# Local attention with a leaky feed-forward layer on one core: sixteen weight combinations put right behind the attention visits, their stores on another queue, and operands computed earlier at the start of a pair

## The chip, the cores and the metric

The kernel runs on one core of a Trainium2 chip. The metric is the device time in microseconds (us) of one execution; lower is better. A profiled execution has a span, from its first to its last instruction, and a time of its own, a little longer than the span.

## The reference

Attention within chunks of 64 positions, for 8 batches, 8 heads, 576 positions and a head dimension of 64, and behind it a feed-forward layer (512 to 2048 to 512) with a leaky rectifier of one slope per hidden unit:

```python
scores = scale * np.matmul(q_c, k_c.transpose(0, 1, 2, 4, 3))      # in each chunk of 64
scores = scores - np.max(scores, axis=-1, keepdims=True)
attn = np.exp(scores)
attn = attn / (np.sum(attn, axis=-1, keepdims=True) + 1e-09)
out = np.matmul(attn, v_c)
...
x = out.transpose(0, 2, 1, 3).reshape(B * S, H * D)                # 4608 tokens x 512
h = x @ w_in
g = np.maximum(h, 0.0) + alpha * np.minimum(h, 0.0)
return g @ w_out
```

All data are float32.

## The kernel before

**Tiling.** The 4608 tokens are nine blocks of 512. One "sub" of attention is 128 tokens (two chunks, all heads), so a block needs four subs, 36 in all. To keep float32 accuracy with a faster matmul, each operand is split into a high and a low part (cast on ScalarE, subtraction on VectorE), and each product takes three passes: high x high, high x low, low x high.

**Two ways for the feed-forward layer.** The first three blocks (PLAIN) are computed plainly: 48 steps, one per block and hidden tile of 128 units. A step is twelve matmuls of 128x128x512 for the first product (`ffn_in`, L318), the rectifier `prelu` (L308, L309 on ScalarE, L310 on VectorE), the split of its result (L330, L331), and twelve matmuls for the second product (`ffn_out`, L343), which run a step or two later. Blocks 0 and 1 are done in turns, so their sums leave PSUM in the middle and are added to a partial sum in DRAM later. The other six blocks go as three pairs, each by a Strassen-like scheme with seven products of half size instead of eight: `first_product` (L598) for eight hidden tiles j, then `second_product` (L714) with seven groups i of eight operands.

**Combinations.** That scheme needs sums and differences of quarters of the weights. `combine(side, j, early)` makes them for `w_in` ("wi") and `w_out` ("wo"), eight hidden tiles each, so sixteen calls. A call adds the parts of two split weights into two tiles "t1" (L499), does four half-width additions on them (L506 to L509), splits the two results (L515 on ScalarE, L516 on VectorE) into staging buffers, and stores four halves of 256 KB to DRAM with `keep_a` (L477), from where the pairs stream them back later (`stream`, L536, on GpSimd's queue). The staging buffers are taken in turn from "raw" (two) and "more" (one); with `early` true only from "raw". "more" is also needed by two of the four copies at a block's end.

**Order of the work.** The combinations run in the loop over the 48 steps. A half-step is the place before `ffn_in(n)` (2n) or behind it (2n + 1). `COMBINE` lists the steps n of the sixteen calls, all at 2n. `visits` lists the half-steps of attention: a visit computes the values of an older sub (L279) and the scores (L201) and softmax (L217 to L225) of a new one; then `attn_blocks` transposes its probabilities on VectorE into a tile with one buffer (L232) and eight stores on SyncE's queue rearrange it into "pT" (L239). Loads of v (L170) also go there. Combinations are held behind the softmax of the visit emitted last by `issue_after`, on VectorE and on ScalarE.

A planner puts each engine's instructions in order from the program's order, priorities and its own estimate of the times; on the chip each engine then runs its list in that order. `high_priority(offset=HIGH)` lets instructions go ahead of HIGH (300) others. TensorE's instructions keep the program's order from step 20 on.

**A block's end.** `store` copies four PSUM banks (L372) into "more" (two halves), "ob" and "g", and adds them to the partial sums in DRAM with accumulating stores on GpSimd's queue (L377). TensorE needs the banks again for the next block. Such ends lie at half-steps 52 and 66.

**A pair's second product.** Its operands are made by `operand(g, at)`, at = 0 to 55: a value or difference of the pair's activations, split (`split`, L554 and L555) into two buffers, which for at % 4 are "t1" twice (0), the halves of "more" (1), or "gh" and "gl" (2 and 3). They are made AHEAD (2) places before their use; the first two are made ahead of the last first product. `first_product` uses "gh" and "g" for sums, and "gl" for the input (L630) of two of its last activations.

Of the kernel before, what the change touches and what calls it, by code (L numbers as in the profile page):

```python
# [10 lines left out]
F32R = mybir.dt.float32r  # L11
# [16 lines left out]
def tile_local_attention_prelu_ffn(  # L28
# [12 lines left out]
    nc = tc.nc  # L41
    P = 128
# [9 lines left out]
    TB = 512  # L52
# [4 lines left out]
    JF = NF // 2  # L57
    EARLY = 2 * SPB
    TURNS = (3, 9)
    HIGH = 300  # L60
# [5 lines left out]
    gp = ctx.enter_context(tc.tile_pool(name="gp", bufs=2))  # L66
    stage = ctx.enter_context(tc.tile_pool(name="stage", bufs=2))
# [5 lines left out]
    def f32(t):  # L73
        return t.bitcast(F32)
# [77 lines left out]
    stages = {}  # L152
# [319 lines left out]
        at = ORDERS[side].index(i)  # L472
        return divmod(7 * j + at if side == "wi" else JF * at + j, 2)

    def keep_a(side, i, j, a):
        n, u = unit(side, i, j)
        nc.gpsimd.dma_start(out=units[side][n][:, u], in_=f32(a))  # L477

    halves = (slice(0, 2 * P), slice(2 * P, 4 * P))

# [10 lines left out]
    def combine(side, j, early):  # L491

        ws = wi if side == "wi" else wo
        pair = [ws[j], ws[JF + j]]
        left, right = halves
        a = []
        for w in pair:
            t = stage.tile([P, 512], F32, name="t1")
            nc.vector.tensor_tensor(t, f32(w[:, 0]), f32(w[:, 1]), op=ALU.add)  # L499
            a.append(t)  # L500
        a11, a22 = a[0][:, left], a[1][:, right]
        if side == "wi":
            a12, a21 = a[0][:, right], a[1][:, left]
        else:
            a21, a12 = a[0][:, right], a[1][:, left]
        nc.vector.tensor_tensor(a22, a21, a22, op=ALU.add)  # L506
        nc.vector.tensor_tensor(a21, a11, a21, op=ALU.subtract)
        nc.vector.tensor_tensor(a11, a22, a11, op=ALU.subtract)
        nc.vector.tensor_tensor(a12, a12, a11, op=ALU.subtract)  # L509
        names = ((2, 4), (3, 1)) if side == "wi" else ((2, 3), (4, 1))  # L510
        for t, name in zip(a, names):
            which = "raw" if early else ("raw", "raw", "more")[fetched[0] % 3]
            fetched[0] += 1
            w = stage.tile([P, 2, 512], F32R, name=which, bufs=2 if which == "raw" else 1)
            nc.scalar.copy(w[:, 0], t)  # L515
            nc.vector.tensor_tensor(w[:, 1], t, f32(w[:, 0]), op=ALU.subtract)  # L516
            for half, s in zip((left, right), name):
                keep_a(side, {1: 5, 2: 6, 3: 7, 4: 3}[s], j, w[:, :, half])

    sequence = [(side, n) for _ in range(NPAIR) for side in ("wi", "wo") for n in range(7 * JF // 2)]  # L520
    ring = []
# [130 lines left out]
    def operand(g, at):  # L652
        i, j = ORDERS["wo"][at // JF], at % JF
        b11, b12, b21, b22 = pieces(g, j)
        if i == 7:
            t = gp.tile([P, TB], F32, name="g")
            with tc.issue_after(behind[0][1].ins):
                nc.vector.tensor_tensor(t, b22, b12, op=ALU.subtract)
        else:
            t = {1: b11, 3: b22, 2: b21}.get(i, b12)  # L660
        if at % 4 == 1:
            both = stage.tile([P, 2, TB], F32R, name="more", bufs=1)
            hi, lo = both[:, 0], both[:, 1]
        else:
            pool, names = (stage, ("t1", "t1")) if at % 4 == 0 else (gp, ("gh", "gl"))
            hi, lo = (pool.tile([P, TB], F32R, name=name) for name in names)
        behind[:] = behind[1:] + [split(t, hi, lo)]
        return hi, lo

    def second_product(g, b, operands, conversion, end):  # L670
# [24 lines left out]
        for i in ORDERS["wo"]:  # L695
# [8 lines left out]
            for j in range(JF):  # L704
                at = JF * ORDERS["wo"].index(i) + j
                if at + AHEAD + EARLIER < 7 * JF:
                    difference(g, at + AHEAD + EARLIER)
                if at + AHEAD < 7 * JF:
                    operands.append(operand(g, at + AHEAD))
                hi, lo = operands.pop(0)  # L710
                w = weight("wo", i, j)
                for m in range(2):
# [36 lines left out]
        for n, name in enumerate(("xh", "xl")):  # L749
            x[b + n] = xp.tile([P, NK, TB], F32, name=name)  # L750

    COMBINE = (20, 22, 23, 24, 26, 29, 30, 31, 33, 35, 36, 37, 39, 40, 41, 43)
    combined = [(side, j) for side in ("wi", "wo") for j in range(JF)]
    ops, conversion = {}, []
    for n, (p, b, f) in enumerate(steps):
# [25 lines left out]
        if ready < NF:  # L781
            prepare(ready, done_x.get({2: SPB, 3: SPB + 2, 4: SPB + 3}.get(ready)))
            ready += 1
        elif n in COMBINE:

            with tc.issue_after(stages["softmax"][0].ins), tc.issue_after(stages["softmax"][1].ins):
                combine(*combined.pop(0), n in (23, 24, 25, 26, 32, 33, 34))
        if n == len(steps) - 8:
            ops, conversion = convert(PLAIN)
        if len(steps) - 8 <= n < len(steps) - 4:  # L790
# [1 line left out]
        pending.append((acc, ffn_in(x[b], f), f, f0, f1, b, False))  # L792
        if 2 * n + 1 in late:
            visit(*late[2 * n + 1])
        if n >= len(steps) - 3:

            with tc.issue_after(stages["split"][0].ins):
                for _ in range(3):
                    conversion.pop(0)()
# [12 lines left out]
    for pair in range(NPAIR):  # L812
        b = PLAIN + 2 * pair
        more = pair + 1 < NPAIR
        if more:
            new_raw(b + 2)
        g = {}
        for j in range(JF):
            if more:
                new += 1  # L820
                visit(new - 2, new if new < NSUB else None)
            if j == JF - 1:
                operands = [operand(g, at) for at in range(AHEAD)]
            first_product(ops, g, j)
        if more:
            ops, conversion = convert(b + 2)
        second_product(g, b, operands, conversion, not more)
# [39 lines left out]
```

## Time and profile before

| | before |
|---|---|
| median of 3 runs | 848.83 us (847.81 to 851.46) |
| profiled execution, its own time | 848.08 us |
| its span | 846.3 us |
| mean granted TensorE clock | 0.988 |
| TensorE (PE) busy | 808.6 us (96%) |
| VectorE (DVE) busy | 670.9 us (79%) |
| ScalarE (ACT) busy | 545.5 us (64%) |
| GpSimd (POOL) busy | 213.0 us (25%) |
| DMA moved | 192.40 MB, mean 227 GB/s |

How to read it: L12 is line 12 of the kernel before. A row of a group gives line, engine, operation, written and read tiles, count, durations. A row of waits gives who waited, then what released it, the total in us, how often, and the longest. A row in order of time gives the start, the duration and the instruction; in brackets the engine's idle time before it and what ended it. "SPq", "ACTq" and so on are the engines' sequencers, here where they issue DMAs. "Issue" is time in which an engine waited for nothing that the profile shows. A DMA's row gives the KB of each and the median us from issue to landing. "t" in the rows is a staging tile ("t1", or "t3" for the transposed probabilities).

The first 40 us load and compute the first attention block; the plain blocks with visits and combinations run to about 349 us; the three pairs follow, with their second products from 437, 608 and 765 us.

### The profile page before, as it was taken

Reading aid. Unit: us, or ns where it says so; the run is one execution under the profiler, and the core shown is the slowest. Engines: PE = TensorE matmul, PEld = TensorE weight load, DVE = VectorE, ACT = ScalarE, POOL = GpSimd, SP = SyncE. Lnnn points to the kernel's source line nnn. Section 1 sums busy time; section 2 is a strip of 40 time slices with the busy share of each in tenths; the row PEclk is TensorE's granted clock in tenths of the full one; section 3 lists DMA queues with packets and bytes.
Section 4 is the critical chain, followed back from the end, with each engine's and each line's share of the span. In section 5 each row is a group of like instructions: output and inputs, shape, how many; then the busy total and the mean of one; then the engine's idle time right before and its main releaser. Section 6 shows DMA issues by size and latency. Waiting matters only on the chain.

```text
span 846.3 us, 15382 instructions
## 1 busy us (share of the span) xinstructions
PE 808.6 (96%) x5248; PEld 646.1 (76%) x5248; DVE 670.9 (79%) x1267; ACT 545.5 (64%) x1392; POOL 213.0 (25%) x339
## 2 busy tenths in 40 slices
PE   4699999999798999999989999999999999999998
PEld 4567888777576778777767877777887888888886
DVE  5798999978797987676778997676789966568875
ACT  6976676656666767678775564877766546556552
POOL 3006222224244331111111242111122421112232
PEclk8999999999899999999999999999999999999999
DMA  9729787558678667687774789876567995555778
GB/s 274 212 76 332 242 257 262 175 169 214 192 234 225 203 215 259 215 259 258 255 260 149 242 221 326 276 253 225 175 209 234 240 310 181 192 186 188 244 218 236
DMA packets 74942, 192.40 MB, mean 227 GB/s; under 512 B 11888, under 2 KB 19056, under 8 KB 74736
## 3 DMA queue, kind: packets, MB, share of 16 engines
q0 software_dynamic: 38240, 127.42, 47.7%
q1 hardware_dynamic: 28480, 49.44, 18.5%
q10 hardware_dynamic: 8144, 14.56, 5.5%
q8 instruction: 42, 0.69, 0.3%
q14 instruction: 36, 0.29, 0.1%
HBM read 135.27 MB, written 42.99 MB: 211 GB/s over the span
## 4 chain that ended last, share of the span: by engine, by line
PE 66%; ACT 9%; DMA 9%; DVE 8%; SPq 4%; issue 3%; ACTq 0%; DVEq 0%; POOL 0%
PE ps_o L714 15%; PE ps_o L598 12%; PE ps_h L714 12%; PE ps_o L343 9%; PE ps_h L318 9%; PE ps_h L598 6%; SPq L239 4%; DMA pT<-t 4%; ACT pr L221 3%; DVE t L232 1%; DMA wi_a<-raw 1%; DMA v_sb<-v 1%; DMA more<-w_in 1%; PE ps_a L279 1%; DVE raw L516 1%
## 5 line engine op out<-in xcount | busy, mean ns | idle before, releaser
L343 PE MATMUL ps_o<-wo,gh 128*128 128x512 f32 x384 | 115.2, 396 | 3.2 <-ACT more L372 3.2
L318 PE MATMUL ps_h<-xh,wi 128*128 128x512 f32 x384 | 106.6, 402 | 3.0 <-DVE g L310 2.3
L318 PEld LDWEIGHTS ps_h<-xh,wi 128*128 128x128 f32 x384 | 71.9, 190 | 21.0 <-DVE g L310 2.9
L343 PEld LDWEIGHTS ps_o<-wo,gh 128*128 128x128 f32 x384 | 71.6, 188 | 20.9 <-ACT more L372 3.6
L221 ACT ACTIVATE pr<-ps_a,mx 128x64 f32<-128x64 f32 x224 | 67.2, 327 | 30.2 <-DVE mx L218 22.8
L343 PE MATMUL ps_o<-wo,gl 128*128 128x512 f32 x192 | 69.8, 395 | 0.0
L598 PE MATMUL ps_o<-wi,raw 128*128 128x512 f32 x171 | 67.9, 397 | 0.0
L598 PE MATMUL ps_o<-wo,raw 128*128 128x512 f32 x171 | 67.8, 396 | 0.0
L318 PE MATMUL ps_h<-xl,wi 128*128 128x512 f32 x192 | 54.0, 400 | 0.0
L221 ACT ACTIVATION_READ_ACCUMULATOR pr<-ps_a,mx 128x1 f32 x224 | 49.3, 220 | 0.0
L554 ACT CAST gh<-wi 128x512 fp32r<-128x512 f32 x48 | 29.9, 623 | 29.4 <-PE ps_o L714 15.1
L308 ACT ACTIVATE wo<-gh 128x512 f32<-128x512 f32 x24 | 15.2, 634 | 51.5 <-DVE gh L621 51.5
L536 POOL DMA_DIRECT2D raw<-wi_a x42 | 22.4, 532 | 103.0 <-PE ps_o L598 61.6
L536 POOL DMA_DIRECT2D raw<-wo_a x42 | 22.3, 532 | 91.9 <-PE ps_o L714 48.6
L318 PEld LDWEIGHTS ps_h<-xl,wi 128*128 128x128 f32 x192 | 36.6, 191 | 8.8
L330 ACT CAST gh<-g 128x512 fp32r<-128x512 f32 x48 | 29.8, 622 | 20.4 <-DVE g L310 15.3
L343 PEld LDWEIGHTS ps_o<-wo,gl 128*128 128x128 f32 x192 | 36.1, 188 | 8.7
L598 PE MATMUL ps_o<-wi,wo 128*128 128x512 f32 x99 | 39.3, 397 | 0.0
L598 PE MATMUL ps_o<-wo,wo 128*128 128x512 f32 x99 | 39.1, 395 | 0.0
L308 ACT ACTIVATE g<-ps_h 128x512 f32<-128x512 f32 x48 | 29.5, 614 | 13.9 <-PE ps_h L318 13.6
L598 PEld LDWEIGHTS ps_o<-wo,raw 128*128 128x128 f32 x171 | 32.2, 188 | 7.7
L598 PEld LDWEIGHTS ps_o<-wi,raw 128*128 128x128 f32 x171 | 32.1, 188 | 7.6
(242 smaller groups left out, 2281.5 us busy)
## 6 DMA issues: line engine op xcount, KB each, us to landing
raw<-wi_a POOLq DMA_DIRECT2D x42, 512.0 KB, 4.8
raw<-wo_a POOLq DMA_DIRECT2D x42, 512.0 KB, 4.5
wi<-wi_a POOLq DMA_DIRECT2D x21, 512.0 KB, 4.9
wo<-wi_a POOLq DMA_DIRECT2D x21, 512.0 KB, 4.6
wi<-wo_a POOLq DMA_DIRECT2D x21, 512.0 KB, 4.1
wo<-wo_a POOLq DMA_DIRECT2D x21, 512.0 KB, 4.2
v_sb<-v SPq DMA_DIRECT2D x28, 256.0 KB, 5.1
pT<-t SPq DMA_DIRECT2D x224, 32.0 KB, 3.7
```

Source lines behind the costliest of these rows:

```text
L221: last = nc.scalar.activation(pr[:, g], one, AF.Exp, bias=mx[:, g], scale=SCALE, accum_out=sm[:, g])
L232: nc.vector.transpose(tb.rearrange("p j h t -> p h j t"), pr)
L239: nc.sync.dma_start(out=pT[dst, i].rearrange("p h t -> p (h t)"), in_=tb[src, j].rearrange("p h t -> p (h t)"),)
L279: pe(nc.tensor.matmul(att[c][par * C:(par + 1) * C, hp * C:(hp + 1) * C], lhsT=v_sb[rows, h * C:(h + 1) * C], rhs=p[rows, :, par * NP + hp ...
L308: nc.scalar.activation(g, h, AF.Relu, scale=-1.0)
L318: pe(nc.tensor.matmul(hps, lhsT=wi[f][:, l, k * P:(k + 1) * P], rhs=xx[:, k], start=(i == 0 and k == 0), stop=(i == 2 and k == NK - 1),))
L330: nc.scalar.copy(gh, g)
L343: pe(nc.tensor.matmul(o, lhsT=a[:, ts], rhs=wo[f][:, l], start=(f == first and i == 0), stop=(f == last and i == 2),))
L536: streamed[0] = nc.gpsimd.dma_start(out=f32(t), in_=units[side][n])
L554: hi = nc.scalar.copy(t_hi, t)
L598: pe(nc.tensor.matmul(ps, lhsT=w[:, l, k * P:(k + 1) * P], rhs=xx[:, xl], start=first and at == 0, stop=at == n - 1, skip_group_check=not ...
L714: pe(nc.tensor.matmul(ps[m], lhsT=w[:, l, m * P:(m + 1) * P], rhs=xx, start=i != 6 and j == 0 and n == 0, stop=j == JF - 1 and n == 2, ski ...
```

## The change

1. The stores of a combination are issued on SyncE's queue instead of GpSimd's (`keep_a` takes a queue). The other callers of `keep_a` stay on GpSimd.
2. The places of the sixteen combinations are now half-steps, 43 to 81 instead of 40 to 86. Twelve stand one half-step behind a visit, four (48, 52, 62, 72) one further. The call is made at both half-steps of a step, and no longer depends on the weights' preparation.
3. `early`, that is leaving "more" alone, holds at half-steps 47 to 55 and 61 to 68 (nine calls); before it held for four calls.
4. In a pair's second product, operand 2 is made ahead of the last first product with the first two, into "gh" and "ob"; operands 3 (into both buffers of "g") and 4 are made one place earlier than before and with a priority offset of 2 x HIGH. From at = 3 on, everything is made as far ahead as before.

```diff
-    def keep_a(side, i, j, a):
+    def keep_a(side, i, j, a, queue=nc.gpsimd):
         n, u = unit(side, i, j)
-        nc.gpsimd.dma_start(out=units[side][n][:, u], in_=f32(a))
+        queue.dma_start(out=units[side][n][:, u], in_=f32(a))
...
-                keep_a(side, {1: 5, 2: 6, 3: 7, 4: 3}[s], j, w[:, :, half])
+                keep_a(side, {1: 5, 2: 6, 3: 7, 4: 3}[s], j, w[:, :, half], nc.sync)
...
-        if at % 4 == 1:
+        if at == 2:
+            hi, lo = gp.tile([P, TB], F32R, name="gh"), stage.tile([P, TB], F32R, name="ob", bufs=1)
+        elif at == 3:
+            hi, lo = (gp.tile([P, TB], F32R, name="g") for _ in range(2))
+        elif at % 4 == 1:
...
-                if at + AHEAD < 7 * JF:
-                    operands.append(operand(g, at + AHEAD))
+                ahead = at + AHEAD + (at < 2)
+                if at != 2 and ahead < 7 * JF:
+                    with tc.high_priority(offset=2 * HIGH) if at < 2 else nullcontext():
+                        operands.append(operand(g, ahead))
...
-    COMBINE = (20, 22, 23, 24, 26, 29, 30, 31, 33, 35, 36, 37, 39, 40, 41, 43)
+    COMBINE = (43, 47, 48, 51, 52, 55, 58, 61, 62, 65, 68, 71, 72, 75, 78, 81)
+    def combine_at(place):
+        if place in COMBINE:
+            with tc.issue_after(stages["softmax"][0].ins), tc.issue_after(stages["softmax"][1].ins):
+                combine(*combined.pop(0), 47 <= place <= 55 or 61 <= place <= 68)
...
-        elif n in COMBINE:
-            with tc.issue_after(stages["softmax"][0].ins), tc.issue_after(stages["softmax"][1].ins):
-                combine(*combined.pop(0), n in (23, 24, 25, 26, 32, 33, 34))
+        combine_at(2 * n)
...
         if 2 * n + 1 in late:
             visit(*late[2 * n + 1])
+        combine_at(2 * n + 1)
...
             if j == JF - 1:
-                operands = [operand(g, at) for at in range(AHEAD)]
+                operands = [operand(g, at) for at in range(AHEAD + 1)]
             first_product(ops, g, j)
```

## The prediction

> **What bounds the kernel now.** I read the page's busy line first, then the waits of PE, then PE's busy time stretch by stretch, then the order of time on the engines around the stretches where PE stands.
>
> ```profile
> PE 808.6 (96%) x5248; PEld 646.1 (76%) x5248; DVE 670.9 (79%) x1267; ACT 545.5 (64%) x1392; POOL 213.0 (25%) x339
> 160.00:325.00 165.00, 154.35 (x1406) 122.44 (x1405) 136.39 (x297) 107.41 (x363) 57.96 (x78) 0.98 0.68 204
> 440.00:445.00 5.00, 2.46 (x8) 1.65 (x7) 3.92 (x7) 4.41 (x8) 0.53 (x1) 0.82 0.63 203
> PE ps_a L279 <- issue: 4.7, 1, 4.7
> PE ps_o L343 <- ACT more L372: 3.2, 1, 3.2
> PE ps_h L318 <- DVE g L310: 1.6, 1, 1.6
> PE ps_a L279 <- DVE xl L305: 0.6, 1, 0.6
> PE ps_a L279 <- ACT more L515: 0.5, 1, 0.5
> PE ps_o L714 <- DVE gl L555: 2.7, 2, 2.5
> ```
>
> TensorE is the bound, so only PE's holes and slow spots can be won. The second and third rows are of busy time by stretch: its bounds, its length, busy PE, PE's weight loads, VectorE, ScalarE, GpSimd, then PE's granted clock, the DMA engines' busy share and GB/s. The second is the stretch of the combinations (PE 154.4 of 165 us, VectorE 136.4). The five waits behind the short stretch are all of PE's waits between 190 and 360 us: 4.7 + 3.2 + 1.6 + 0.6 + 0.5 = 10.6 us. The last row is all of them between 400 and 500 us, at the start of the first pair's second product.
>
> **What each hole costs**, from the order of time on PE (start, duration), and one row of the chain for the normal pace:
>
> ```profile
> 206.67 0.69 PE L279 MATMUL ps_a<-pT,v_sb 64*64 64x64 f32 x32
> 207.77 0.74 PE L343 MATMUL ps_o<-wo,gh 128*128 128x512 f32 x2
> 216.04 0.40 PE L343 MATMUL ps_o<-wo,gl 128*128 128x512 f32 x1
> 221.17 0.31 PE L279 MATMUL ps_a<-pT,v_sb 64*64 64x64 f32 x2 [4.73 <-issue]
> 224.01 2.07 PE L318 MATMUL ps_h<-xh,wi 128*128 128x512 f32 x4
> 228.78 0.63 PE L343 MATMUL ps_o<-wo,gh 128*128 128x512 f32 x2
> 313.75 2.79 PE ps_h L318 x12
> 440.17 0.39 PE L714 MATMUL ps_o<-gh,raw 128*128 128x512 f32 x1
> 443.10 0.73 PE L714 MATMUL ps_o<-gl,raw 128*128 128x512 f32 x1 [2.54 <-DVE gl L555]
> 447.48 1.56 PE L714 MATMUL ps_o<-t,wi 128*128 128x512 f32 x6
> ```
>
> An undisturbed visit takes 207.77 - 206.67 = 1.1 us, and twelve large matmuls 2.8 us. Hole A: from 216.44 to 224.01 are 7.6 us for one visit, 6.5 lost; the twelve matmuls after it take 4.8 instead of 2.8, 2.0 lost; 8.4 us in all. Hole B, a block's end, is the 3.2 us on L372. Holes C and D are 0.5 and 1.6. Hole E: twelve matmuls from 440.17 to 447.48 take 7.3 instead of 2.8 us, 4.5 lost, of which only 2.5 is the wait; the rest is the granted clock, 0.82 in that window. All five make 18.2 us, the most that this change can win.
>
> The Trainium skill (TensorE: Matmul & The Clock Gate, Part 1) says that a clock window is about 3.4 us and that an idle window is needed for the slow clock. By that, removing hole E's 2.5 us wait need not give back the slow part, and E would be worth 2.5; the rows above show the slow clock behind a 2.5 us wait, so here the trace disagrees, and the sum below does not use the rule.
>
> **Part 1: a pair's operands (hole E).** Rows of VectorE, and PE's only wait after 500 us:
>
> ```profile
> 437.54 1.28 DVE L630 TENSOR_TENSOR gl<-ps_h,g 128x512 f32<-128x512 f32 x2
> 441.15 0.69 DVE L310 SCALAR_TENSOR_TENSOR wi<-gl,wi 128x512 f32<-128x512 f32 x1 [0.92 <-ACT wi L309]
> 442.36 0.68 DVE L555 TENSOR_TENSOR gl<-wi,gh 128x512 fp32r<-128x512 f32 x1
> 442.96 0.68 DVE L310 SCALAR_TENSOR_TENSOR wi<-ps_o,wi 128x512 f32<-128x512 f32 x1
> PE ps_o L714 <- DVE gl L555: 0.2, 1, 0.2
> ```
>
> The two instructions of L630 fill both "gl" buffers with the inputs of the last activations. The first is free after L310 at 441.15; only then, at 442.36, is operand 2's low half written there, while PE wanted it at 440.17 + 2.8 / 12 = 440.4. The change puts that half into the single "ob" buffer, which no store needs then, and computes operand 2 ahead of the last first product. Operand 3 goes into the two "g" buffers and operand 4 moves one place ahead; both get priority over the activations. No instruction is added: each operand is one cast and one subtraction as before. What is late next: operand 3 is used first at 441.6 and its second "g" is free after L630, at 438.8; operand 7 is the result of the activation that ends with L310 at 442.96 to 443.6, needs a cast and a subtraction of about 0.6 us each, and is wanted 5 x 1.4 us after operand 2, at 447.2. Some 2.4 us are spare there, of which the casts of operands 3 and 4 put ahead take 1.2. The operand of i = 7 that reuses "g" comes after operand 3 is eaten (443.0) and is wanted near 448.6. I take 4.0 of the 4.5 us. The later pairs have no such hole, as the last row says, and gain nothing. Bounds: 0, where the wait only moves to operand 5, 6 or 7, to 4.5.
>
> **Part 2: the stores on SyncE's queue.** 64 stores of 256 KB leave GpSimd's queue.
>
> ```profile
> L477 POOL DMA_DIRECT2D wi_a<-raw x24: 725/725/753, 180.4 to 248.4; - x24
> L170 SPq DMA_DIRECT2D v_sb<-v x28: 328/526/1590, 126.2 to 581.3; - x28
> L239 SPq DMA_DIRECT2D pT<-t x224: 507/588/1925, 173.8 to 591.3; - x112
> 295.11 7.63 SPq L239 DMA_DIRECT2D pT<-t  x8
> 200.05 1.74 POOL L377 DMA_DIRECT2D partial<-more  x2 [0.89 <-ACT more L372]
> partial<-v_sb SPq DMA_DIRECT2D x2, 256.0 KB, 4.2
> 204.83 8.18 DMA wi_a<-raw
> 210.36 0.62 ACT L515 CAST raw<-t 128x512 fp32r<-128x512 f32 x1 [3.17 <-DMA wi_a<-raw]
> 213.09 0.62 ACT L515 CAST raw<-t 128x512 fp32r<-128x512 f32 x1 [2.11 <-DMA wi_a<-raw]
> 217.35 0.31 ACT L221 ACTIVATE pr<-ps_a,mx 128x64 f32<-128x64 f32 x1 [2.38 <-DVE mx L218]
> ```
>
> GpSimd has work or an issue in 58 of the 165 us, so the 64 x 0.73 us that it is spared are worth nothing by themselves; what it does beside them in this stretch, the accumulating stores of block ends and the first loads of the weight stream, comes no later. The landing is what counts. Hole A's chain: the accumulating stores go to GpSimd's queue at 200.05, the combination's stores follow on the same queue and one takes 8.18 us; ScalarE's casts into occupied "raw" buffers wait until 210.36 and 213.09; VectorE's subtraction behind the cast stands ahead of the maximum of a visit whose scores were ready at 207.8; the softmax starts at 217.35, with PE idle since 216.4. A plain 256 KB store of partial sums on SyncE's queue took 4.2 us. With 4.2 for 8.2 the last cast comes 4.0 us earlier, so of PE's wait of 5.4 us 1.4 is left, and of the 2.0 us of slow matmuls behind it, with so short a hole, I leave half. Hole A gives 6.0 of 8.4 us. Bounds of a landing: 4.2 to 8.2, so 0 to 8.4 for the hole.
>
> The cost is on SyncE: 64 x 0.53 = 34 us of issue (v_sb, of the same size and all 128 partitions, is the nearest row; its ends of 0.33 and 1.59 us make 21 and 102), beside eight pT stores in each visit (8 x 0.59 = 4.7 us, 7.6 when crowded). While a store waits there for its subtraction, the next visit's v_sb load and pT stores stand behind it; for pT wait that visit's values on PE two visits on, and the transpose L232 of the visit after (its buffer is single).
>
> The Trainium skill (DMA: Bandwidth & Descriptors, Issuing engines are not separate DMA queues) speaks against this part: all issuers share the same 16 DMA engines, and starting transfers on another one saves only its issue time. By that the landing stays at 8.2 us, hole A stays, and the gain is 5 us instead of 11. What that does here is rival 1.
>
> **Part 3: the places and the spared third buffer.** Counting half-steps, the sixteen combinations move from 40 to 86 to 43 to 81: twelve right behind a visit, four a half-step later. Nine instead of four leave "more" alone, those round the block ends at half-steps 52 and 66.
>
> ```profile
> 249.10 1.45 POOL L477 DMA_DIRECT2D wi_a<-more  x2
> 256.35 1.15 ACT L372 COPY more<-ps_o 128x512 f32<-128x512 f32 x2
> 160.00:325.00 165.00, 21.12 (x32) 0.98 0.68 204
> 160.00:325.00 165.00, 6.72 (x16) 0.98 0.68 204
> 160.00:325.00 165.00, 21.15 (x32) 0.98 0.68 204
> 304.75 0.71 DVE L232 STREAM_TRANSPOSE t<-pr 128x512 f32<-128x512 f32 x1 [2.71 <-DMA pT<-t]
> ```
>
> Hole B: a combination's stores leave "more" at 249.10 to 250.6, and the two copies of the block's end that need it come at 256.35, when PE has stood for 3 us. With "more" spared at 61 to 68 they can follow the copy into "ob" near 251. I take 3.0 of 3.2 us; bounds 0 (another instruction keeps ScalarE) to 3.2.
>
> The price is density. The three rows of busy VectorE are a combination's additions (L499, 21.1 us), one of its four half-width operations (6.7, the others alike) and its subtractions (L516, 21.2): 21.1 + 4 x 6.7 + 21.2 = 69.1 us for sixteen. The rest of VectorE's 136.4 us is 67.3, over 165 - 13.7 = 151.3 us of undisturbed time. The 38 half-steps from 43 to 81 last 38 x 2.8 + 11 visits x 1.1 = 118.5 us; in them VectorE would have 69.1 + 67.3 x 118.5 / 151.3 = 121.8 us to do, 103%. So the combinations cannot all stay behind their visits; some slip beyond 81, where there is room, and VectorE's queue is full on the way. Holes C and D are what such a full queue costs now: in D, L232 waited 2.7 us for pT, L310 stood behind it, and PE lost 1.6. I let C and D double, from 2.1 to 4.1 us: 2.0 lost. Bounds: 2.1 gained (both go) to 17.6 lost (D's 1.6 us in each of eleven visits).
>
> **The sum.** 4.0 + 6.0 + 3.0 - 2.0 = 11.0 us off the profiled execution's 848.08 (span 846.3) is 837.1; that execution is 0.75 below the median of the runs, so I predict 838 us for the median.
>
> **Rivals.**
> 1. The landing stays slow. For: the accumulating stores of 200.05 move the same bytes whoever issues the others, and five combinations in a row now share two buffers. Against: 4.2 us on the other queue. A gains nothing: 4.0 + 3.0 - 2.0 = 5.0, 843.8 us.
> 2. E's wait moves to operand 5, 6 or 7, since ScalarE has the casts of 3 and 4 ahead of the activations. Against: 1.2 us spare. The rest stays: 7.0, 841.8 us.
> 3. Slower: SyncE's queue becomes the bound. With crowded pT stores, 11 x (7.6 + 0.5) + 34 = 123 us of issue stand in the 118.5; pT lands late, L232 waits in each visit, L310 behind it, PE after that: 11 x 1.6 = 17.6 lost against 4.0 + 6.0 + 3.0 won makes 853.4 us. It decides from about eleven such waits on, or from stores at the upper end of 1.59 us. Against: at 0.59 us a pT store, the same sum is 91 us.
> 4. The combinations do not move: VectorE is full, so they run where they ran, and holes A to D stay. Only E goes: 4.0, 844.8 us.
>
> **How the numbers follow.** Chances: forecast 0.40, rival 1 0.22, rival 2 0.13, rival 3 0.10, rival 4 0.15. Half a per cent (4.2 us, about what a measurement of this kernel tells from no change) puts the bounds at 844.6 and 853.1. Below 844.6 lie nearly all of the forecast and rival 2 (0.51), two thirds of rival 1 (0.14) and a third of rival 4 (0.05): 0.70. Rival 3 is the slower side, 0.10; 0.20 is left. The forecast's own range is 833 to 842, from A gaining 2 to all of it. The range for the time is 831 to 850: the low end is nearly all of the 18.2 us, the high end leaves out rival 3 and little else.
>
> **What would show it.** Right: no wait on "gl" L555 near 440 and a granted clock of 1.00 there; no PE wait on L372 at the second block's end; casts L515 that wait less than 1.5 us for a store; landings of wi_a and wo_a stores from SyncE near 4 us. Wrong: L515 still waiting 3 us or more on "raw" (rival 1), a PE wait on L555 after 441 (rival 2), L232 waiting on pT in most visits or pT stores issued more than 8 us after their transpose (rival 3), L499 rows still spread to 313 us (rival 4).

## The result and the profile after

The changed kernel takes 857.8 us (median of 6 runs, 853.65 to 859.25), the kernel before beside it 851.78 (6 runs, 847.81 to 852.58): a ratio of 1.0092, with a 95% interval of 1.0065 to 1.0119 (the quotient of these two medians alone, 1.0071, lies inside it). It is 0.9% slower, where 1.3% faster was forecast, and the time lies above the range. The profiled execution is the longest of the six (859.25 us, span 857.5).

From the page of the changed kernel, the busy line; then its two busiest queues, with packets, MB and their share of 16 engines:

```profile
PE 813.0 (95%) x5248; PEld 650.6 (76%) x5248; DVE 672.5 (78%) x1267; ACT 544.1 (63%) x1392; POOL 166.5 (19%) x275
q0 software_dynamic: 33120, 110.64, 41.3%
q1 hardware_dynamic: 45888, 66.22, 24.3%
```

GpSimd is spared 46.5 of its 213.0 us, as told, and PE is busy for a smaller share of a longer span: there are more holes. They are in the waits of PE between 160 and 460 us (line, wait, us in total, times, longest), and in PE's busy time by stretch (the columns of the prediction's stretch rows):

```profile
PE ps_o L343 <- ACT more L372: 9.8, 1, 9.8
PE ps_a L279 <- ACT xl L295: 6.8, 1, 6.8
PE ps_a L279 <- issue: 2.2, 1, 2.2
PE ps_a L279 <- DVE xl L305: 0.6, 1, 0.6
```

```profile
240.00:280.00 40.00, 30.20 (x239) 23.84 (x238) 28.80 (x62) 22.81 (x79) 3.46 (x4) 0.87 0.80 229
325.00:360.00 35.00, 30.37 (x177) 24.71 (x178) 30.45 (x57) 25.16 (x70) 1.64 (x3) 0.85 0.68 224
456.00:461.00 5.00, 5.00 (x23) 4.09 (x22) 4.60 (x8) 4.42 (x9) 1.06 (x2) 1.00 0.68 220
461.00:466.00 5.00, 5.00 (x24) 4.05 (x23) 4.96 (x9) 3.42 (x7) 1.06 (x2) 1.00 0.53 189
```

Hole B, at the second block's end, has grown from 3.2 to 9.8 us. A new hole of 6.8 us stands at the last combinations; I call it F. Hole A's wait has shrunk from 4.7 to 2.2 us. Hole E is gone: the second product starts at 453.3 us now, 456 to 466 is the same stage as 440 to 450 before, and there PE is busy throughout at a clock of 1.00, with no wait on L555. In the stretches of B and F the mean granted clock is 0.87 and 0.85, where the whole stretch of the combinations had 0.98 before, so each hole costs more than its wait.

Stage by stage, the span grew by 11.2 us. Start to the scores of the visit at 160 us: 3.5 more (160.49 to 163.98), though the engines' lists are the same up to there in all eighteen kernels of this document; these reached it at 159.1 to 164.9 us, so this part is scatter between executions. From there to the first product (L598): 189.5 to 201.8, or 12.4 more. First product: 87.4 in both. From the second product to the end: 408.9 to 404.2, or 4.7 less. The change won at hole E and lost 12.4 us where the combinations are. Of these, 8.8 are PE's waits (19.4 in the rows above, against 10.6 before); the rest goes with the lower clock.

**How the loss arises.** In order of time on VectorE, SyncE and ScalarE (start, duration), behind the first block's end:

```profile
203.27 1.83 SPq L477 DMA_DIRECT2D wi_a<-raw  x2
208.54 0.65 DVE L516 TENSOR_TENSOR raw<-t,raw 128x512 fp32r<-128x512 f32 x1
208.65 5.75 SPq L239 DMA_DIRECT2D pT<-t  x8
213.14 0.62 ACT L515 CAST raw<-t 128x512 fp32r<-128x512 f32 x1 [4.64 <-DMA wi_a<-raw]
214.49 0.53 SPq L170 DMA_DIRECT2D v_sb<-v  x1
215.12 2.35 SPq L477 DMA_DIRECT2D wi_a<-raw  x4
```

A tile was ready at 209.2 (208.54 + 0.65). Its first store was issued at 215.1, because in SyncE's list they stand behind the eight pT stores of the visit and its v_sb load. The queue did not wait there: it was busy with pT. Pairing the end of each of the 32 subtractions L516 with the issue of the later of its two stores, the median of this lateness is 5.1 us in the changed kernel and 1.0 in the one before (4.1 and 1.4 in the mean); 21 of the 32 are later than 3 us, against 1. A staging buffer is free only when its stores have landed, so it is held some 4 us longer in the median, and the combinations spread: the last of their additions (L499) starts at 334.2 us instead of 314.9.

The landing did not become shorter either. Of the two stores issued by SyncE from 203 to 206 us (KB each, us from issue to landing; the trace has the landing of one of the two):

```profile
wi_a<-raw SPq DMA_DIRECT2D x2, 256.0 KB, 9.1
```

That is 9.1 us on SyncE's queue, beside the block's adding stores, where GpSimd's four took 6.8 to 8.2 in the kernel before.

Hole B in ScalarE's and PE's order, and the store between:

```profile
251.70 0.59 ACT L372 COPY ob<-ps_o 128x512 f32<-128x512 f32 x1 [0.40 <-issue]
253.21 0.62 ACT L515 CAST more<-t 128x512 fp32r<-128x512 f32 x1 [0.92 <-DVE t L509]
255.64 1.93 SPq L477 DMA_DIRECT2D wi_a<-more  x2
262.85 1.07 ACT L372 COPY more<-ps_o 128x512 f32<-128x512 f32 x2 [2.39 <-DMA wi_a<-more]
263.49 1.22 PE L343 MATMUL ps_o<-wo,gh 128*128 128x512 f32 x2 [9.80 <-ACT more L372]
```

The seventh combination (place 58, the one between the block ends that may use the third buffer) has slipped by a visit. Its cast into "more" now stands behind the block's copy into "ob" and ahead of the two copies into "more". Those have to wait until its stores have landed, and PE waits for them. The second of these stores is issued 2.2 us after its tile is ready and takes 6.1 us to land. But the cast itself starts only 0.5 us before PE begins to wait, so with stores that leave at once and land as slowly I estimate from these rows that 8 of the 9.8 us would be left. The place of the cast is set by ScalarE's list, which the planner made before the kernel ran: the combination slipped there, and not on the chip.

Hole F, the same in small: the second store of a tile, at 318.11, stands behind pT and v_sb, 6.6 us after its tile was ready, and takes 7.1 us to land; the next cast into "more" waits for it on ScalarE, ahead of the softmax of the visit that PE wants.

```profile
318.11 0.44 SPq L477 DMA_DIRECT2D wo_a<-more  x1
325.32 0.62 ACT L515 CAST more<-t 128x512 fp32r<-128x512 f32 x1 [7.00 <-DMA wo_a<-more]
329.63 1.33 PE L279 MATMUL ps_a<-pT,v_sb 64*64 64x64 f32 x29 [6.85 <-ACT xl L295]
```

### The profile page after: what moved, and what is told of

Same layout as the page of the kernel before. It is cut to its first block, busy times and chain, and to the rows that moved or that the text cites. A ratio compares the mean times of both kernels' runs of the same rounds, so it can differ in the third digit from the quotient of the medians.

```text
span 857.5 us, 15388 instructions
## 1 busy us (share of the span) xinstructions
PE 813.0 (95%) x5248; PEld 650.6 (76%) x5248; DVE 672.5 (78%) x1267; ACT 544.1 (63%) x1392; POOL 166.5 (19%) x275
## 4 chain that ended last, share of the span: by engine, by line
PE 75%; DMA 10%; DVE 8%; ACT 4%; issue 2%; SPq 1%; DVEq 0%; ACTq 0%
PE ps_o L598 19%; PE ps_o L721 15%; PE ps_h L721 11%; PE ps_o L343 10%; PE ps_h L598 9%; PE ps_h L318 9%; DMA wi_a<-raw 3%; DMA wi<-kT 2%; PE ps_a L279 1%; DMA raw<-w_in 1%; ACT pr L221 1%; DVE t L499 1%; DVE gl L331 1%; PE ps_a L201 1%; DMA wi<-wo_a 1%
## 5 line engine op out<-in xcount | busy, mean ns | idle before, releaser
L343 PE MATMUL ps_o<-wo,gh 128*128 128x512 f32 x384 | 119.5, 409 | 9.8 <-ACT more L372 9.8
L343 PEld LDWEIGHTS ps_o<-wo,gh 128*128 128x128 f32 x384 | 74.5, 196 | 28.3 <-ACT more L372 10.2
L343 PE MATMUL ps_o<-wo,gl 128*128 128x512 f32 x192 | 71.3, 402 | 0.0
L598 PE MATMUL ps_o<-wi,raw 128*128 128x512 f32 x171 | 67.9, 397 | 0.0
L598 PE MATMUL ps_o<-wo,raw 128*128 128x512 f32 x171 | 67.8, 397 | 0.0
L554 ACT CAST gh<-wi 128x512 fp32r<-128x512 f32 x45 | 28.1, 625 | 25.2 <-PE ps_o L721 10.9
L343 PEld LDWEIGHTS ps_o<-wo,gl 128*128 128x128 f32 x192 | 37.0, 192 | 8.9
L598 PE MATMUL ps_o<-wi,wo 128*128 128x512 f32 x99 | 39.4, 397 | 0.0
L598 PE MATMUL ps_o<-wo,wo 128*128 128x512 f32 x99 | 39.1, 395 | 0.0
L217 DVE TENSOR_REDUCE mx<-ps_a 128x4 f32<-128x256 f32 (+1 forms) x64 | 26.5, 450 | 15.7 <-PE ps_a L187 10.3
L598 PEld LDWEIGHTS ps_o<-wo,raw 128*128 128x128 f32 x171 | 32.2, 188 | 7.7
L598 PEld LDWEIGHTS ps_o<-wi,raw 128*128 128x128 f32 x171 | 32.1, 188 | 7.6
```

What stands on the lines that cost most here:

```text
L217: nc.vector.tensor_reduce(mx[:, at], part, axis=AX.X, op=ALU.max)
L343: pe(nc.tensor.matmul(o, lhsT=a[:, ts], rhs=wo[f][:, l], start=(f == first and i == 0), stop=(f == last and i == 2),))
L554: hi = nc.scalar.copy(t_hi, t)
L598: pe(nc.tensor.matmul(ps, lhsT=w[:, l, k * P:(k + 1) * P], rhs=xx[:, xl], start=first and at == 0, stop=at == n - 1, skip_group_check=not ...
```

## The experiments

Each experiment is timed against the kernel before on the same chip; one execution of each is profiled. "Late" is the median lateness of a tile's stores as above, "B" the PE wait of L343 on L372 (a copy into "more", or into the tile in brackets), "last" when the last of the combinations' additions starts.

| kernel | ratio, 95% interval | late, us | B, us | last, us |
|---|---|---|---|---|
| before | 1 | 1.0 | 3.2 | 314.9 |
| changed | 1.0092 (1.0065 to 1.0119) | 5.1 | 9.8 | 334.2 |
| operands alone | 0.9964 (0.9940 to 0.9987) | 1.2 | 3.4 | 312.6 |
| changed, old operands | 1.0132 (1.0095 to 1.0169) | 4.7 | 8.9 | 330.6 |
| changed, stores on GpSimd | 0.9945 (0.9924 to 0.9966) | 1.0 | 0.2 (g) | 315.7 |
| SyncE stores alone | 1.0120 (1.0087 to 1.0154) | 5.0 | 20.0 | 326.8 |
| places alone | 0.9993 (0.9974 to 1.0012) | 1.0 | 0.2 (g) | 313.5 |
| changed, stores ahead of pT | 0.9974 (0.9954 to 0.9994) | 1.0 | none | 324.7 |
| changed, pT on GpSimd | 0.9989 (0.9969 to 1.0009) | 0.4 | 3.4 (ob) | 299.7 |
| changed, half the stores | 0.9939 (0.9916 to 0.9962) | 4.0 | none | 317.4 |
| the same, ahead of pT | 0.9987 (0.9971 to 1.0003) | 0.3 | 8.8 | 324.3 |
| operands, half the stores | 0.9945 (0.9926 to 0.9964) | 0.7 | 4.8 | 317.3 |
| half, seventh in raw | 0.9980 (0.9958 to 1.0002) | 2.4 | 1.3 (g) | 331.5 |
| changed, plain partial stores | 1.0026 (1.0009 to 1.0044) | 4.7 | 8.9 | 323.6 |
| changed, last in raw | 1.0029 (1.0010 to 1.0048) | 4.2 | 9.8 | 332.0 |
| changed, seventh in raw | 1.0170 (1.0148 to 1.0192) | 3.5 | none | 350.3 |
| changed, both in raw | 1.0194 (1.0168 to 1.0220) | 3.2 | none | 349.8 |
| changed, all in raw | 1.0201 (1.0168 to 1.0234) | 3.3 | none | 353.3 |

Lateness does not rank the kernels: half the stores is 4.0 us late and the fastest, half ahead of pT is 0.3 us late and has hole B again. And whenever the queue or the place of a store changes, the planner makes other lists for ScalarE and VectorE too, from some place between 180 and 200 us on. Such a run changes both at once, what is late on the chip and what stands where. Of the runs in which stores leave or land at another time, only that with plain partial stores keeps all lists.

### Which part it is

**Operands alone**: the diff's hunks in `operand` and `second_product`, and nothing else, put into the kernel before.

> The kernel before with the operands alone (operand 2 into "ob", 3 into "g", 3 and 4 one place earlier). Both theories: the wait of 2.5 us on "gl" and the slow clock behind it go, 4.5 us in all, so a ratio of 0.995 to the kernel before. If the gain seen at the pair's start in the changed kernel came from elsewhere (the different end of the plain part), the ratio is 1.00.

0.9964: 3.1 us faster (0.0036 x 849), with no wait on L555 left at the start of the second product.

**The changed kernel without them**: those hunks undone.

> The changed kernel without the operands' part, so stores on SyncE and the new places and flags. Both theories: 4.5 us longer than the changed kernel, about 12 us longer than before, a ratio of 1.014. If the parts hang together (the pair's start waits for nothing once the plain part ends later), it is as long as the changed kernel, 1.009.

1.0132, and the wait is back (`L555`, 1.8 us). The difference to 1.0092 is 3.4 us. Both ways round the operands are worth 3 to 3.5 us. A third pair below, the places with and without the operands on GpSimd's queue (0.9945 and 0.9993), gives 4.1. Each of the three is open by 2 us or more.

**The changed kernel with its stores back on GpSimd's queue**: one argument.

```
-                keep_a(..., j, w[:, :, half], nc.sync)
+                keep_a(..., j, w[:, :, half])
```

> The changed kernel with the combinations' stores back on GpSimd's queue. Queue theory (the stores stand behind eight pT stores and a load of v on SyncE, so the staging buffers come free some 6 us later): the 12 us lost between the first visit and the pairs shrink to 2 or less, ratio 0.992 to 0.998. Place theory (the combinations slip, and the one that still uses "more" falls on the block's end): TensorE's wait of 9.8 us on the copy into "more" stays, ratio 1.004 to 1.010.

0.9945, faster than before. This one argument is worth 1.5% (1.0092 to 0.9945, 12.5 us): without the other queue there is no loss.

**The kernel before with its stores on SyncE's queue**: the same argument, put in.

> The kernel before with the stores on SyncE's queue alone, old places and flags, old operands. Queue theory: 8 to 12 us longer, ratio 1.010 to 1.014, with casts that wait for stores more than the 5.3 us of before. Place theory: within 2 us of before, ratio 0.998 to 1.002.

1.0120 with nothing else changed in the program. Its waits show hole B at both block ends, and ScalarE's order why, here at the first:

```profile
PE ps_o L343 <- ACT more L372: 20.0, 2, 11.8
206.73 0.62 ACT L515 CAST raw<-t 128x512 fp32r<-128x512 f32 x1 [3.11 <-DMA wi_a<-raw]
208.08 1.07 ACT L372 COPY more<-ps_o 128x512 f32<-128x512 f32 x2
```

The copies into "more" do not wait for a store themselves. They stand in the list behind a cast that waits for a late one; in the kernel before they come ahead of this cast, at 199.2 us.

**The places and flags alone**, on GpSimd's queue with the old operands.

> The kernel before with the new places and flags of the combinations alone; the stores stay on GpSimd's queue and the operands are as before. Theory: between the run with operands and places on GpSimd's queue (0.9945) and the run with the operands alone (0.9964) the places are worth about 0.2%: 0.996 to 1.000, about 847 us; a staging tile's stores are issued within 1 to 2 us of its end, as in the kernel before. Rival: the places are worth nothing or hurt without the third buffer near the second block end: 1.000 to 1.005.

0.9993 (0.9974 to 1.0012): not to be told from nothing. Holes A and B are both gone there, with the stores still on GpSimd's queue, but a new wait stands at the visit behind the second block end, and another of 1.6 us for "k_sb":

```profile
258.11 1.02 PE L279 MATMUL ps_a<-pT,v_sb 64*64 64x64 f32 x27 [4.25 <-DMA pT<-t]
```

PE's waits between 190 and 360 us are 8.8 us, against 10.6 before. With "more" free, the block end's four adding stores go out from 248.8 to 252.3 us instead of 251.3 to 259.1, beside the last pT stores of a visit. The last two of these land in 6.4 and 7.6 us, against 4.4 and 5.4 in the kernel before. That the adding stores slow them fits the run with plain partial stores below, but no run shows it here.

### What it is about the queue

**Stores ahead of pT**: still all on SyncE, with a priority that puts them ahead of most of a visit's pT stores in SyncE's list.

```
-        queue.dma_start(out=units[side][n][:, u], in_=f32(a))
+        with tc.high_priority(offset=2 * HIGH) if queue is nc.sync else nullcontext():
+            queue.dma_start(out=units[side][n][:, u], in_=f32(a))
```

> The changed kernel with its 64 combination stores still on SyncE's queue, but given a high priority, so that the planner writes them ahead of most of a visit's eight pT stores (first three to eight rows of pT behind them) instead of behind. Theory O, the order within the queue is what costs: the 1.5% between this queue and GpSimd's (857.8 against 843.2) mostly goes: 843 to 849, ScalarE's casts L515 wait on staging buffers under 6 us in sum (after: 10.9 on raw and 7.0 on more), hole L343 under 4 (after 9.8). Rival D, the cost is that queue's own stores (landing, packets, issue time) wherever they stand: 855 to 860. Rival P, the pT rows now come late by four issues of 0.6 us and the visits pay: L279 waits on DMA pT by over 5 us in sum and the time is 850 to 856.

0.9974, as the theory of the order said: 1.2% of the 1.5% is back with the same stores on the same queue. The seventh combination does not slip here, and hole B is gone. SyncE's order, and what PE pays for it:

```profile
235.13 0.87 SPq L478 DMA_DIRECT2D wi_a<-raw  x2
236.10 0.51 SPq L239 DMA_DIRECT2D pT<-t  x1
236.72 1.07 SPq L478 DMA_DIRECT2D wi_a<-raw  x2
237.84 4.31 SPq L239 DMA_DIRECT2D pT<-t  x7
PE ps_a L279 <- DMA pT<-t: 6.6, 2, 4.7
```

(The edit adds a line, so L477 is L478 here.) The stores leave 1 us after their tile. PE waits for pT instead, as the third theory had it, 6.6 us in two waits, both at the visit behind the second block end. But 3.6 to 4.3 us of wait for pT stand at that visit with the stores on GpSimd's queue too, so some 3 us are left to the new order, and 2.5 us (0.3%) do not come back.

**pT on GpSimd**: L239 issued by `nc.gpsimd`, the stores on SyncE.

> The changed kernel with the eight pT stores of each late visit (L239) issued by GpSimd, so that on SyncE's queue the combination stores stand behind v_sb and the weight loads alone. Theory O (order behind pT): casts wait under 6 us in sum for staging buffers and the time is 843 to 850, less whatever pT loses on GpSimd behind the accumulating stores of the block ends (L279 on DMA pT). Rival D (the queue itself): 855 to 860 with the cast waits still there. If pT suffers on GpSimd, L279 waits on DMA pT near the block ends by over 5 us, and the time tells less than the cast waits.

0.9989: the loss is gone in this way too, with lateness at 0.4 us. The casts still waited 14.0 us in sum for landings (8.8 and 5.2), more than the 6 I gave the theory, but the holes B (into "more") and F are not there. The planner made other lists for it (VectorE's from 180 us on), so this run, like the one before it, supports the order as the cause without isolating it.

**Half the stores**: of each tile's two stores one on SyncE, one on GpSimd.

```
-                keep_a(..., w[:, :, half], nc.sync)
+                keep_a(..., w[:, :, half], nc.sync if half is left else nc.gpsimd)
```

> The changed kernel with only one of each staging tile's two stores on SyncE (the left half), the other on GpSimd: 32 and 32. Theory O: a staging buffer is free only when both stores have landed, so the store that stands behind pT still sets it; the time stays near the changed kernel's, 853 to 858, and the cast waits stay over 10 us in sum. Rival D (a price per store on that queue: 1.5% / 64 each): half of it goes, 849 to 852. Rival L (it is SyncE's issue time, 0.4 to 0.6 us a store, that delays pT): as D.

0.9939, better than any theory's number. I had taken the lists to stay as they were. Lateness did stay: 17 of the 32 tiles are later than 3 us (21 in the changed kernel), 12 under 0.5 us (6), and the median is 4.0. What changed is that the seventh combination did not slip, and that no cast into "more" waits for a late store at the end. In ScalarE's order its cast into "more" stands a visit earlier, and the block's copies find the buffer free:

```profile
239.63 0.62 ACT L515 CAST more<-t 128x512 fp32r<-128x512 f32 x1 [1.96 <-DMA q_sb<-qT]
247.89 1.08 ACT L372 COPY more<-ps_o 128x512 f32<-128x512 f32 x2 [0.41 <-PE ps_o L343]
```

**Plain partial stores**: the adding at the block ends taken away, with every engine's list as in the changed kernel.

```
-                nc.gpsimd.dma_start(out=before, in_=ob, accum_op=ALU.add)
+                nc.gpsimd.dma_start(out=before, in_=ob)
```

> The changed kernel with the block ends' adding stores (L377) made plain stores; it leaves out the addition of the second weight block's sums to the first's. The order of all five engines' instructions is that of the changed kernel. Theory T, the adding keeps the DMA engines busy and so lengthens the landings of the stores that SyncE issues at the same time: the pair issued at about 203 us lands in 4 to 5 us instead of 9.1, the cast that waited 4.6 us for it (213.1 us) waits under 1.5 us; whole time 848 to 855. Rival U, it is the mere traffic of a block end: 7 to 9 us as before and 854 to 859.

1.0026, 0.7% below the changed kernel. The pair of stores behind the block's end (issued at 199.75 us here) and the cast that waits for it:

```profile
wi_a<-raw SPq DMA_DIRECT2D x2, 256.0 KB, 6.1
206.48 0.62 ACT L515 CAST raw<-t 128x512 fp32r<-128x512 f32 x1 [2.13 <-DMA wi_a<-raw]
```

The landing is 6.1 instead of 9.1 us and the cast's wait 2.1 instead of 4.6: between the two theories. About 3 us of this slow landing is the adding; some 2 over the 4.2 us of a plain store in a quiet time remain. Hole B stays (8.9 us), as the lists are the same, and so does F (5.6).

### By which way late stores cost

**All combinations in the two raw buffers**: the flag is True everywhere.

```
-                combine(*combined.pop(0), 47 <= place <= 55 or 61 <= place <= 68)
+                combine(*combined.pop(0), True)
```

> The changed kernel with every combination casting into the two raw buffers, so that the third buffer (more) is never held by a combination and the block ends' copies (L372) and the operands find it free. Theory B, the late stores cost through that buffer: the hole at the second block end (9.8 us at L343) and the one at the last combination (6.85 us at L279 behind the cast into more, which waited 7.0 us) go, and little comes in their place: 843 to 848. Rival R, the casts then wait for the two raw buffers as long as they waited for the three: L515 on raw rises from 10.9 to over 15 us, casts slip further, and the time is 852 to 860.

1.0201, slower than either theory said. Holes B and F are gone, but the additions slip to 353.3 us and another hole, of 15.8 us, comes in their place. The weight stream's loads need the raw buffers too: in the run with the seventh alone kept out (below), where GpSimd issues such a load, and PE's wait for it:

```profile
354.51 0.53 POOL L536 DMA_DIRECT2D raw<-wi_a  x1 [2.42 <-DMA wo_a<-raw]
PE ps_o L598 <- DMA raw<-wi_a: 13.0, 2, 10.7
```

**The seventh combination alone kept out of "more"** (`47 <= place <= 68`), everything ahead of it as in the changed kernel:

> The changed kernel with the seventh combination (place 58) also kept out of the third buffer; everything ahead of it is ordered as in the changed kernel. Theory B, the hole at the second block end (9.8 us at L343) is there because this combination slips a visit and then holds the third buffer when the block's copies L372 want it: the hole goes, L343 waits under 2 us for L372, and the time is 848 to 852. Rival R, without the third buffer it and all that follow wait for the two raw ones and slip on, until the last ones meet the first product's loads (L598 waiting on raw<-wi_a, 15.8 us where no combination used the third buffer): 855 to 865.

1.0170. Hole B closes, and the rival happens: one buffer fewer, the last additions at 350.3 us, and the first product waits 10.7 us for its first load (13.0 in all). So this run does not give hole B's price.

**Those from place 75 on kept out of "more"**:

> The changed kernel with the combinations from place 75 on also kept out of the third buffer; the order ahead of them is the changed kernel's, the hole at the second block end stays (9 to 10 us). Theory F, the wait of L279 at 329.6 us (6.85 us, behind the cast into the third buffer that waited 7.0 us for a store standing behind pT) goes: 850 to 853. Rival R: the last combinations slip instead and the first product waits for its loads: 857 to 865.

1.0029: hole F goes, B stays, and 0.6% (5.3 us) comes back; 850.8 us, within what was expected. F's price is measured.

**Both**:

> The changed kernel with the seventh combination and those from place 75 on kept out of the third buffer. If the two holes are what the late stores cost and nothing takes their place: 841 to 846. If the casts then slip as with no use of the third buffer: 858 to 867, with L598 waiting over 8 us for raw<-wi_a.

1.0194, with L598 waiting 15.9 us: as with no use of "more" at all.

**Half the stores, ahead of pT**:

> The changed kernel with one of each tile's two stores on SyncE, placed ahead of pT by priority, and the other on GpSimd: both late issue and long queues taken away. Theory O (time goes with how late the stores are issued): every tile's stores issued within 2 us of its end, no worse than the half-and-half run without priority: 0.991 to 0.995, 840 to 844. Rival P (each store ahead of pT delays pT, and pT sets the visits): 0.995 to 0.999, with L279 waiting for DMA pT by over 4 us in sum.

0.9987: against the theory, which made the time go with the lateness alone, as the half-and-half run already was. The lateness is the least of all (0.3 us) and PE never waits for pT, so that the number fell into the rival's range without the rival's sign. But the seventh combination stands behind the block's end again, and hole B is there (the edit adds a line, so the cast L515 is L516 here):

```profile
251.37 0.70 ACT L516 CAST more<-t 128x512 fp32r<-128x512 f32 x1
256.33 1.07 ACT L372 COPY more<-ps_o 128x512 f32<-128x512 f32 x2 [2.48 <-DMA wi_a<-more]
PE ps_o L343 <- ACT more L372: 8.8, 1, 8.8
```

To the run without this hole (0.9939) it is 0.5%, 4.1 us. So hole B needs no late store: it follows from the cast's place in ScalarE's list. Why the planner puts the seventh there though the stores leave early stays open.

**The old places with the operands and half the stores**, and **the new ones with half the stores and the seventh in raw**:

> The kernel before (old places and flags) with the earlier operands, and one of each tile's two stores on SyncE, the other on GpSimd. If the half-and-half stores are worth something of themselves, this is faster than the operands alone (0.9964): 0.991 to 0.995. If what made half-and-half good was the new places with it, or if it was no better than all on GpSimd: 0.995 to 1.000, with the late issues (over 3 us) of some tiles back and L343 waiting for L372 by over 3 us.

> The half-and-half stores (one of each tile's two on SyncE, one on GpSimd) with the new places and the earlier operands, and the seventh combination kept out of the third buffer. That kernel had no hole at L343, so nothing is gained there: 0.992 to 0.997, 842 to 846, the same as without the flag within the interval. Rival: with one buffer fewer the casts around the second block end wait (L515 on raw over 8 us in sum) and it is slower: 0.997 to 1.003.

0.9945 and 0.9980. The first has the time of its first theory with the signs of the second (13 of the 32 tiles later than 3 us, 4.8 us at L343). It is as fast as the new places (0.9939 and 0.9945), and its interval overlaps that of the operands alone (0.9964): half-and-half and the places add nothing that can be told apart. The second is the rival's case: L515 on raw waits 11.8 + 7.6 us, and where there was no hole nothing is gained.

The best three, 0.9939 to 0.9945, beat both kernels: the earlier operands, with the stores on GpSimd or split over both queues. None of them can be told from the operands alone.

## Why the prediction was wrong

**What bounds the kernel, holes A to E.** Right in place: the change moved the time only at such holes and at new ones.

**Part 1, operands.** Right. 4.0 of hole E's 4.5 us was the term; 3.1, 3.4 and 4.1 us are measured, inside its bounds. The order told (operand 2, 3 and 4 early, 5 to 7 in time) held, and rival 2 did not come: no wait on L555 is left at the second product's start, and the clock is 1.00 where 0.82 stood behind the wait.

**Part 2, the landing.** Wrong. This is the term "with 4.2 for 8.2" of hole A: the landing on the other queue was 9.1 us, above the upper bound that I gave. The nearest row for a 256 KB store on SyncE's queue (4.2) was from a quiet time; the stores in question go out beside a block's adding stores, and the adding makes about 3 us of the landing (6.1 us with the adding taken away). That is rival 1's sentence, and the Trainium skill's rule (DMA: Bandwidth & Descriptors, Issuing engines are not separate DMA queues) holds for the landing, 9.1 against 8.18 us. That rule goes on to say that another issuer saves only the issue time, usually small. It is not all that it changes: the move to another issuer's list cost 1.5% here, and 1.2% came back further ahead in that list. Nor did hole A need a shorter landing: with the new places it is gone on GpSimd's queue too, though a cast there still waits 4.1 us for a store.

**Part 2, the queue.** This step failed, and it decided the sign. I priced the issues on SyncE (34 us; 36.1 are measured) and asked who waits behind a store ("the next visit's v_sb load and pT stores stand behind it"). I did not ask what the stores stand behind. The sum had nothing for it, while the rows were quoted: eight pT stores are 4.7 us, 7.6 when crowded, and v_sb follows. A store that comes in the middle of this is late by up to that much, and its buffer is held as long: 5.1 us in the median instead of 1.0. With the stores on GpSimd's queue the rest of the change is 4.7 us faster than before (0.9945), and with them on SyncE's some 8 slower; the queue cost these 12.5 us, and 10 of them (1.2%) came back with the same stores on the same queue, but ahead of pT. Not all of it is lateness on the chip. Hole F is: 6.6 us late, 7.1 to land, 5.3 us in the time. Hole B comes from the list that the planner made for this queue. No run here holds the lists and moves only the lateness, so how the 12.5 us divide stays open.

**Part 3, the third buffer.** On GpSimd's queue it did what was told: hole B went from 3.2 to 0.2 us with the places alone. But the places alone gave nothing that can be measured: the copies that found "more" free also sent the adding stores out earlier, and beside these a wait of 4.3 us for pT appeared. The sum had no term for that; that the one made the other is not shown. On SyncE's queue the 3.0 us won became 6.6 lost: place 58 is the one between the block ends that may still use "more", and once it slipped it hit the copies. I had written that combinations would slip, and looked only beyond place 81 for what that does. The 2.0 us for a fuller VectorE is not borne out: PE's wait on L310 (1.6 us before) and VectorE's for pT at L232 (4.6 us before, between 160 and 345) are not among the changed kernel's in this stretch.

**Rivals.** Rival 3 had the right sign and the right engine with the wrong mechanism: L232 did not wait for pT, the stores waited behind pT. At 853.4 us, and a chance of 0.10, it was the nearest. Of rival 1 the landing came true, its time did not. Rival 4's sign was there too (additions to 334.2 us), but as lateness: they moved later than before, not nowhere. The range ended at 850 because the only case above it was taken for the tenth to leave out.

**The signs** named beforehand were good ones: no L555 and the full clock (right); L372, casts and landings (wrong); L232 (not seen).

## What to carry to other kernels

When a transfer moves to another issuing queue, read that queue's own order at the time when the transfer becomes ready: what stands ahead of it is added to the time for which its source buffer is held. Count how many buffers turn round on it and find the one place where a slip of one step makes it collide with something else; the price is there, not in the mean lateness. Where a planner orders the engines ahead of time, the collision can stand in its lists already. Take landing times from rows beside the same neighbours, not from the same queue at a quiet time.

## What the runs showed of the hardware

The same 64 stores make more packets on SyncE's queue. Between the page of the kernel before

```profile
q0 software_dynamic: 38240, 127.42, 47.7%
q1 hardware_dynamic: 28480, 49.44, 18.5%
```

and that of the changed kernel, q0 loses 5120 packets and q1 gains 17408: 80 and 272 packets for a store of 256 KB. That alone made no landing longer: put ahead of pT, the stores into wi_a from raw landed in 2.6 us in the median, against 3.4 on GpSimd's queue in the kernel before.

Adding stores slow the others that are in flight with them: with the lists of all engines the same, plain ones gave 1.0026 instead of 1.0092 and a landing of 6.1 instead of 9.1 us.

PE's granted clock was halved behind short waits too. In the kernel before, PE waits 2.54 us until 443.1 us; its granted clock is 0.50 from 443.2 to 446.6 and 1.00 ahead of that and behind it. Behind a wait of 1.89 us in the run with half the stores it is 0.50 from 212.0 to 215.2.
